# The first chunk reordered: dummy matmuls between its first real ones, the first z turn in two banks, the later z turns behind value matmuls, and V's pieces on both transfer queues

## The chip, the cores and the metric

The kernel runs on 1 core of a Trainium2 chip. The metric is the device time of one execution in microseconds. Nearly every run has the record of its granted TensorE clock. A "trace" is the profile of one execution.

The engines are named as in the profile: PE is TensorE, DVE is VectorE, ACT is ScalarE, POOL is GpSimd, SP is SyncE.

## The reference

Eight batches of squared-ReLU attention are gated by `u`, and all rows then go through a two-layer network.

```python
scores = z @ z.transpose(0, 2, 1) / S          # batch 8, S = 3008, z is 64 wide
attn = np.maximum(scores, 0.0) ** 2
x = (u * (attn @ v)).reshape(B * S, 256)
h = x @ w_in                                   # 256 -> 2048
out = (h / (1 + np.exp(-1.702 * h))) @ w_out   # 2048 -> 256
```

## The kernel before

For each batch the kernel takes S in six chunks, five of 512 columns and a last one of 448. Per pair of row blocks it makes scores on PE (`sc`), a ReLU on ACT (`rl`), a square on DVE (`a`), and value matmuls on PE (`o`). As the scores are symmetric, many squared blocks are reused: a DMA transpose on SP's queue turns `a` into `tt`, which later chunks use as weights.

Batch 0 has no batch ahead of it to hide its start. It loads z in groups of four blocks, casts them to 16 bits, turns them with PE transposes into a PSUM bank, and copies the bank to `ZT`. V comes through a staging tile `vst` that POOL casts. Everything below is this start (cuts marked).

```python
def warm_up(n):
    w = ps1.tile([P, CH], F32, name="w", tag="ps1")
    for k in range(n):
        pe.matmul(w, nil[:, :P], nil, start=(k == 0), stop=(k == n - 1))

def first_cast(g, by_act=False):           # zf (f32) -> zst (f16), two copies
    ...
        if by_act:
            act.activation(dst, src, AF.Copy, scale=1.0)
        else:
            dve.tensor_copy(dst, src)

def first_zt(g):                           # four PE transposes, then a copy to ZT
    zp = ps1.tile([P, CB, P], F16, name="zp", tag="ps1")
    for k in range(CB):
        pe.transpose(zp[:, k, :], z2[:, k, :, :], ident)
    def copies():
        ...
        if g != 1:
            act.activation(dst, src, AF.Copy, scale=1.0)
        else:
            dve.tensor_copy(dst, src)
    return copies

def load_u(b, i):                          # four transfers of 128 KB in pieces of 256 bytes
    eng = pool if b or i else sp
    ...

# the order of the start
first_z(0, CB, sp)                         # z group 0
first_z(CB, 2 * CB, act)                   # z group 1
for n0 in (0, VB):
    load_v(0, n0)                          # V blocks 0-3 and 4-7, on ACT's queue
first_z(2 * CB, 4 * CB, sp)                # z groups 2 and 3, ahead of all V on SP's queue
first_z(4 * CB, NJ, sp)
for n0 in range(2 * VB, NJ, VB):
    load_v(0, n0)                          # the rest of V, on SP's queue
warm_up(7)
for g in range(2):
    first_cast(g)
for copies in [first_zt(g) for g in range(2)]:
    copies()
posts = scores(0, [queue.pop(0) for _ in range(2)])
turns = []
for g in (2, 3):
    first_cast(g)
    turns.append(first_zt(g))
for post_ in posts:
    post_()                                # ReLU and square
turns[0]()
take(0, 1)                                 # one more pair of scores
...
# in chunk 0: turns[1]() at step 3; casts of groups 4 and 5 on ACT at steps 7 and 17, turns at 16 and 25
```

## Time and profile before

| | before |
|---|---|
| median of 3 runs (range) | 1192.46 us (1191.73 to 1192.65) |
| span of the profiled run | 1190.8 us |
| PE busy | 1183.7 us |
| PE waiting for other engines' results, in all | 3.3 us, all before 20 us |
| first value matmul | 8.40 us |
| first scores of chunk 1 | 25.14 us |

The busy line of the page (engine, busy us, share of the span, instructions):

```profile
PE 1183.7 (99%) x11427; PEld 722.6 (61%) x11427; DVE 820.6 (69%) x1315; ACT 830.5 (70%) x987; POOL 231.9 (19%) x325
```

PE is the bound, so only PE's idle time and its clock can be won at the start. The view by stretches shows both, in the columns named by its second line. PEclk is the granted clock.

```profile
core 0: us, PE busy (x) PEld busy (x) DVE busy (x) ACT busy (x) POOL busy (x), PEclk, DMA share, GB/s
4.45:7.86 3.41, 1.81 (x20) 0.85 (x18) 2.83 (x7) 2.65 (x4) 1.31 (x2) 1.00 1.09 352
7.86:11.27 3.41, 3.41 (x12) 0.77 (x10) 1.70 (x4) 2.65 (x4) 2.72 (x4) 0.50 1.10 346
11.27:25.00 13.73, 13.26 (x72) 4.66 (x70) 8.98 (x13) 11.82 (x17) 8.64 (x13) 1.00 1.18 205
```

In the first stretch PE was busy 1.81 of 3.41 us; in the next its clock was half, so 12 matmuls filled 3.41 us. The record of the clock begins only with the first full-speed window, at 4.45 us in this trace. Before that PEclk prints 1.00 although the warm-up matmuls start 0.427 us apart, against 0.216 for the same shape later. The timeline (start, us, engine, line, operation, output<-inputs, shape, count, idle time before it and what ended it) shows what PE waited for in the first of them:

```profile
4.72 0.60 ACT L141 ACTIVATE ZT<-zp 128x512 f16<-128x512 f16 x1 [1.21 <-PE zp L133]
5.38 0.61 PE L231 MATMUL sc<-ZT 64*128 64x512 f16 x4 [0.45 <-ACT ZT L141]
5.74 1.73 DVE L126 CAST zst<-zf 128x256 f16<-128x256 f32 x4
7.40 1.28 DVE L259 TENSOR_TENSOR a<-rl 128x1024 f16<-128x1024 f16 x2
7.53 0.40 PE L133 MATMUL zp<-ident,zst 128*128 128x128 f16 x4 [0.84 <-DVE zst L126]
8.40 1.03 PE L331 MATMUL o<-a,V 128*128 128x512 f16 x2
...
25.14 0.61 PE L231 MATMUL sc<-ZT 64*128 64x512 f16 x4
```

DVE casts z of groups 2 and 3 with hardly a wait for data (z landed at 5.72 us, 0.06 us after the copy before was done), then makes the first squares, and the value matmuls follow.

### The profile page before, as it was taken

Reading aid. Unit: us, or ns where it says so; the run is one execution under the profiler, and the core shown is the slowest. Engines: PE = TensorE matmul, PEld = TensorE weight load, DVE = VectorE, ACT = ScalarE, POOL = GpSimd, SP = SyncE. Lnnn points to the kernel's source line nnn. Section 1 sums busy time; section 2 is a strip of 40 time slices with the busy share of each in tenths; the row PEclk is TensorE's granted clock in tenths of the full one; section 3 lists DMA queues with packets and bytes.
Section 4 is the critical chain, followed back from the end, with each engine's and each line's share of the span. In section 5 each row is a group of like instructions: output and inputs, shape, how many; then the busy total and the mean of one; then the engine's idle time right before and its main releaser. Section 6 shows DMA issues by size and latency. Waiting matters only on the chain.

```text
span 1190.8 us, 27541 instructions
## 1 busy us (share of the span) xinstructions
PE 1183.7 (99%) x11427; PEld 722.6 (61%) x11427; DVE 820.6 (69%) x1315; ACT 830.5 (70%) x987; POOL 231.9 (19%) x325
## 2 busy tenths in 40 slices
PE   8999999999999999999999999999999999999998
PEld 3446765467754676546765478554775547855577
DVE  6788755777757775587765877558776487664776
ACT  7887865688656886478864787657876578672785
POOL 5243100331012320133101331014200142001000
PEclk9999999999999999999999999999999999999999
DMA  9996567666787667856778558886579855695012
GB/s 230 175 137 110 127 138 130 86 112 134 143 132 79 107 141 151 130 68 102 158 140 131 72 95 159 157 112 89 104 128 164 115 88 109 138 165 96 1 37 72
DMA packets 373021, 141.80 MB, mean 119 GB/s; under 512 B 315424, under 2 KB 366368, under 8 KB 372896
## 3 DMA queue, kind: packets, MB, share of 16 engines
q1 hardware_dynamic: 314256, 96.77, 45.1%
q0 software_dynamic: 57280, 42.03, 23.0%
q8 instruction: 89, 1.46, 0.5%
q10 hardware_dynamic: 1360, 1.25, 0.3%
q14 instruction: 36, 0.29, 0.1%
HBM read 60.29 MB, written 24.64 MB: 71 GB/s over the span
## 4 chain that ended last, share of the span: by engine, by line
PE 98%; ACT 0%; DMA 0%; DVE 0%; issue 0%; SPq 0%; ACTq 0%
PE o L331 40%; PE hg L372 27%; PE st L473 23%; PE sc L231 6%; PE yp L529 2%; DMA zf<-in_z_dram 0%; ACT rl L245 0%; DVE zst L126 0%; DVE a L259 0%; ACT ZT L141 0%; ACT zst L124 0%; DVE y L489 0%; SPq L109 0%; PE zp L133 0%; ACTq L245 0%
## 5 line engine op out<-in xcount | busy, mean ns | idle before, releaser
L380 ACT ACTIVATE gf<-hg 128x1024 f32<-128x1024 f32 (+1 forms) x384 | 385.8, 1005 | 138.0 <-PE hg L372 114.7
L245 ACT ACTIVATE rl<-sc 128x1024 f16<-128x1024 f32 x309 | 303.5, 1027 | 150.3 <-PE sc L231 147.5
L331 PEld LDWEIGHTS <-V 64*128 64x128 f16 (+1 forms) x4052 | 239.6, 94 | 235.4 <-issue 13.0
L372 PE MATMUL hg<-xt,W 128*128 128x512 f16 (+1 forms) x1408 | 354.6, 374 | 0.0
L384 DVE TENSOR_SCALAR gt<-gf 128x1024 f16<-128x1024 f32 (+1 forms) x320 | 223.2, 698 | 136.8 <-ACT gf L380 134.1
L331 PE MATMUL o<-a,V 64*128 64x512 f16 (+3 forms) x2286 | 303.8, 369 | 0.0
L259 DVE TENSOR_TENSOR a<-rl 128x1024 f16<-128x1024 f16 x274 | 188.7, 693 | 158.5 <-ACT rl L245 158.1
L193 POOL DMA_DIRECT2D uq<-in_u_dram x188 | 128.5, 691 | 612.2 <-PE sc L231 329.1
L331 PE MATMUL o<-tt,V 64*128 64x512 f16 (+1 forms) x1510 | 234.4, 377 | 0.0
L372 PEld LDWEIGHTS <-W 128*128 128x128 f16 x1536 | 139.3, 98 | 119.3 <-issue 2.6
L473 PEld LDWEIGHTS <-gt 128*128 128x128 f16 x2816 | 169.5, 98 | 31.8
L473 PEld LDWEIGHTS <-s 128*128 128x128 f16 x2112 | 127.8, 98 | 25.3 <-issue 0.3
L231 PE MATMUL sc<-ZT 64*128 64x512 f16 (+1 forms) x688 | 121.6, 367 | 1.2 <-ACT ZT L141 0.9
L473 PE MATMUL st<-WT,gt 128*128 128x128 f16 x1408 | 93.0, 219 | 0.0
L473 PE MATMUL st<-WT,s 128*128 128x128 f16 x1408 | 92.3, 219 | 0.0
L473 PE MATMUL st<-W,gt 128*128 128x128 f16 x1408 | 92.3, 219 | 0.0
L489 DVE SCALAR_TENSOR_TENSOR y<-st,uP 128x256 f32<-128x256 f32 x132 | 55.0, 419 | 21.6 <-PE st L473 10.9
L382 ACT ACTIVATE gt<-gf 128x1024 f16<-128x1024 f32 (+1 forms) x64 | 66.0, 1031 | 2.1
L348 DVE TENSOR_TENSOR xt<-o,ut 128x512 f16<-128x512 f32 x80 | 51.4, 683 | 22.7 <-PE o L331 22.7
L231 PEld LDWEIGHTS <-ZT 64*128 64x128 f16 x688 | 39.0, 94 | 45.0 <-issue 9.1
L483 ACT ACTIVATE uP<-st 128x256 f32<-128x256 f32 x132 | 49.7, 377 | 23.2 <-PE st L473 11.2
L446 DVE TENSOR_TENSOR s<-s,gt 128x1024 f16<-128x1024 f16 x88 | 60.3, 685 | 1.0
(51 smaller groups left out, 618.2 us busy)
## 6 DMA issues: line engine op xcount, KB each, us to landing
out_dram<-y SPq DMA_DIRECT2D x40, 512.0 KB, 3.3
uq<-in_u_dram POOLq DMA_DIRECT2D x156, 128.0 KB, 3.6
V<-in_v_dram POOLq DMA_DIRECT2D x35, 256.0 KB, 6.7
tt<-a SPq DMA_TRANSPOSE x232, 3.8
uq<-in_u_dram POOLq DMA_DIRECT2D x32, 112.0 KB, 5.2
vst<-in_v_dram SPq DMA_DIRECT2D x3, 512.0 KB, 5.8
out_dram<-y POOLq DMA_DIRECT2D x4, 384.0 KB, 3.2
zst<-in_z_dram POOLq DMA_DIRECT2D x7, 192.0 KB, 8.2
```

The costliest lines, as they stand in the source:

```text
L193: eng.dma_start(uq[k * QW:(k + 1) * QW, :n // QW].rearrange("t q c k -> t q (c k)"), src[:, :, cs])
L231: pe.matmul(sc[:, r, :m * P], zt[h, 2 * kp + r, :], zt[h, (qi + 1) * CB - m:(qi + 1) * CB, :], start=True, stop=True,)
L245: act.activation(rl, sc, AF.Relu, scale=csc)
L259: dve.tensor_tensor(a, rl, rl, ALU.mult)
L331: ins = pe.matmul(acc[c][:, :n], V16[b][h, j].rearrange("p (c k) -> p k c", k=NCC)[:, c], weights(b, i, j)[h], start=(k, m) == first[c], s ...
L372: pe.matmul(hg[:, e, :n], W1[:, c, ff * P:(ff + 1) * P], XT[b, i][:, c, :n], start=(c == 0), stop=(c == NCC - 1),)
L380: act.activation(gf[:, :, :n], hg[:, :, :n], AF.Gelu_apprx_sigmoid, scale=1.0 / FSC)
L382: act.activation(g, gf[:, :, :n], AF.Copy, scale=FSC)
L384: dve.tensor_scalar(g, gf[:, :, :n], FSC, None, ALU.mult)
L446: dve.tensor_tensor(s_, ST[b, k, "S1", h], a11, ALU.subtract)
L473: pe.matmul(bank[:, m, :], lhs()[:, f, m, :], right[:, ff, :], start=name in ("P1", "P2", "P5") and m == 0 and ff == 0, stop=ff == NFF // ...
L489: dve.scalar_tensor_tensor(y[:, :, o, c], ST[b, k, "bank" + x], 1.0 / FSC, ST[b, k, "after" + u_], ALU.mult, ALU.add,)
```

## The change

The intent: keep PE's clock up with dummy matmuls in the gaps, get the first scores sooner by splitting the first copy, get V's first block sooner by giving half of it to each queue, and let the first value matmuls go ahead of the turns of later z groups. The casts move from ACT to DVE. The core of the diff:

```diff
-    def warm_up(n):
-        w = ps1.tile([P, CH], F32, name="w", tag="ps1")
+    def keep_warm(n):
+        if "w" not in ZT:
+            ZT["w"] = ps1.tile([P, CH], F32, name="w", tag="ps1")
 ...
-            if by_act:
-                act.activation(dst, src, AF.Copy, scale=1.0)
-            else:
-                dve.tensor_copy(dst, src)
+            dve.tensor_copy(dst, src)
 ...
+        if g == 0:
+            zh = [ps1.tile([P, CB // 2, P], F16, name="zh", tag="ps1") for _ in range(2)]
+            ...
+                act.activation(dst[:, 0], zh[0].rearrange("d n p -> d p n"), AF.Copy, scale=1.0)
+                dve.tensor_copy(dst[:, 1], zh[1].rearrange("d n p -> d p n"))
 ...
-            if g != 1:
+            if g > 2:
 ...  load_v, batch 0
-            dst, eng = pa.tile(...), act if n0 < 2 * VB else sp
+            dst, eng = pa.tile(...), sp
+        if b == 0 and n0 == 0:
+            full = VB // 2
+            act.dma_start(dst[:, full:], v[b, full * P:VB * P].rearrange("(n p) c -> p n c", p=P))
 ...
-    FIRST_ZT, FIRST_CAST = {16: 4, 25: 5}, {7: 4, 17: 5}
+    FIRST_ZT, FIRST_CAST = {11: 3, 20: 4, 29: 5}, {2: 3, 15: 4, 24: 5}
-        0: {2: 1, 6: 2, 14: 2, 22: 2, 30: 2, 38: 2},
+        0: {2: 1, 8: 2, 16: 2, 25: 2, 33: 2, 40: 2},
 ...
-    first_z(2 * CB, 4 * CB, sp)
+    first_z(2 * CB, 4 * CB, act)
+    load_v(0, 2 * VB)
     first_z(4 * CB, NJ, sp)
-    for n0 in range(2 * VB, NJ, VB):
+    for n0 in range(3 * VB, NJ, VB):
         load_v(0, n0)
-    warm_up(7)
+    keep_warm(7)
 ...
+    keep_warm(1)
     posts = scores(0, [queue.pop(0) for _ in range(2)])
-    turns = []
-    for g in (2, 3):
-        first_cast(g)
-        turns.append(first_zt(g))
+    first_cast(2)
     for post_ in posts:
         post_()
-    turns[0]()
-    take(0, 1)
+    keep_warm(3)
+    posts = scores(0, [queue.pop(0)])
+    keep_warm(2)
+    ...
+    first_zt(2)()
+    posts[0]()
```

On the two hardware queues, z of groups 2 and 3 now stands behind V's first block and beside the next V blocks. Before, it stood ahead of V on SP's queue.

More of the change, by code (lines that the diff above doesn't have):

```diff
@@ L77 @@
     late, LATE = [], []
+    ZP = {}
     ZT, V16, UQ, UT, XT, unit, TT = {}, {}, {}, {}, {}, {}, {}
@@ L91, in behind @@
         tc.add_manual_dep(m.ins, sig.ins.name, SYNC, reason="row tiles of one bank")
-    def warm_up(n):
-        w = ps1.tile([P, CH], F32, name="w", tag="ps1")
+    def keep_warm(n):
+        if "w" not in ZT:
+            ZT["w"] = ps1.tile([P, CH], F32, name="w", tag="ps1")
         for k in range(n):
-            pe.matmul(w, nil[:, :P], nil, start=(k == 0), stop=(k == n - 1))
+            pe.matmul(ZT["w"], nil[:, :P], nil, start=(k == 0), stop=(k == n - 1))
     def first_z(n0, n1, eng):
@@ L117, in first_z, with first_cast @@
                 eng.dma_start(zf[h * SREM:(h + 1) * SREM, m1 + CB - 1, :], z[0, S0:S])
-    def first_cast(g, by_act=False):
+    def first_cast(g):
         m = g % CB * CB
@@ L122, in first_cast, with copies @@
             dst, src = ZT["st"][g // CB][:, m:m + CB, c, :], ZT["f"][g // CB][:, m:m + CB, :]
-            if by_act:
-                act.activation(dst, src, AF.Copy, scale=1.0)
-            else:
-                dve.tensor_copy(dst, src)
+            dve.tensor_copy(dst, src)
     def first_zt(g):
         z2 = ZT["st"][g // CB][:, g % CB * CB:(g % CB + 1) * CB]
-        zp = ps1.tile([P, CB, P], F16, name="zp", tag="ps1")
+        if g == 0:
+            zh = [ps1.tile([P, CB // 2, P], F16, name="zh", tag="ps1") for _ in range(2)]
+            for k in range(CB):
+                pe.transpose(zh[k // 2][:, k % 2, :], z2[:, k, :, :], ident)
+            def copies():
+                dst = ZT[0][:, :CB, :].rearrange("d n p -> d (n p)").rearrange("d (p h n) -> d h p n", h=2, n=CB // 2)
+                act.activation(dst[:, 0], zh[0].rearrange("d n p -> d p n"), AF.Copy, scale=1.0)
+                dve.tensor_copy(dst[:, 1], zh[1].rearrange("d n p -> d p n"))
+            return copies
+        zp = ZP[g] if g in ZP else ps1.tile([P, CB, P], F16, name="zp", tag="ps1")
         for k in range(CB):
@@ L172, in load_v @@
         if b == 0:
-            dst, eng = pa.tile([P, VB, D], F32, name="vst", tag="tt", bufs=14), act if n0 < 2 * VB else sp
+            dst, eng = pa.tile([P, VB, D], F32, name="vst", tag="tt", bufs=14), sp
         full = min(VB, NJ - 1 - n0)
+        if b == 0 and n0 == 0:
+            full = VB // 2
+            act.dma_start(dst[:, full:], v[b, full * P:VB * P].rearrange("(n p) c -> p n c", p=P))
         eng.dma_start(dst[:, :full, :], v[b, n0 * P:(n0 + full) * P].rearrange("(n p) c -> p n c", p=P))
-        if full < VB:
+        if n0 + VB == NJ:
             for h in range(2):
@@ L605 @@
         copies()
+    keep_warm(1)
     posts = scores(0, [queue.pop(0) for _ in range(2)])
-    turns = []
-    for g in (2, 3):
-        first_cast(g)
-        turns.append(first_zt(g))
+    first_cast(2)
     for post_ in posts:
         post_()
-    turns[0]()
-    take(0, 1)
+    keep_warm(3)
+    posts = scores(0, [queue.pop(0)])
+    keep_warm(2)
+    for g in (2, 3):
+        ZP[g] = ps1.tile([P, CB, P], F16, name="zp", tag="ps1")
+    first_zt(2)()
+    posts[0]()
     load_u(0, 1)
@@ L630 @@
                     load_u(0, 0)
-                if b == 0 and i == 0 and n == 3:
-                    turns[1]()
                 if b == 0 and i == 0 and n in FIRST_CAST:
-                    first_cast(FIRST_CAST[n], True)
+                    first_cast(FIRST_CAST[n])
                 if b == 0 and i == 0 and n in FIRST_ZT:
```

## The prediction

> **What bounds the kernel.** The tensor engine: the page's busy line gives PE 1183.7 of 1190.8 us. The list of waits shows PE waiting for other engines' results only before 20 us, 3.3 us in all. In the view by stretches, PE idles 2.8 us before 12 us and 3.7 us in the last 11; the change touches the first only. The same view grants PE a clock of 0.50 from 8 to 11 us (0.86 and 0.72 in the half microseconds on either side), 1.00 elsewhere: one slow stretch of some 3.4 us. In it value matmuls start 0.427 us apart, not 0.216. The Trainium skill, "TensorE: Matmul & The Clock Gate", Part 1, tells of such a gate: full clock after a busy window of about 3.4 us, half after an idle one. The trace agrees: from 4.5 to 7.5 us PE was busy 1.4 of 3.0.
>
> **What changes.**
> 1. Six 512-column dummies (0.216 us each) enter gaps where PE waits for ACT or DVE. They cost almost nothing and make that window about two thirds busy. If the clock holds, eight matmul slots gain 0.21 us each, 1.7 us; about 1 counts, since ACT (relu 1.02) and DVE (square 0.69) also pace these steps.
> 2. The first z turn's copy, 0.60 on ACT, becomes halves of some 0.38 on ACT and DVE: first scores at 5.15 instead of 5.37, 0.2 us.
> 3. ACT, busy 9.8 of 11 us from 12 to 23, loses the casts of groups 4 and 5 (1.4 us) and group 2's copy (0.60); DVE takes them. But the chain of scores, two relus (1.94), z copy (0.55) and next scores takes about 2.95 us, longer than eight value matmuls with scores (2.5). It occurs for groups 3, 4 and 5, before for two, leaving 0.2 to 0.5 us of PE idle time each. Net gain 0.4.
> 4. V's first block, on both queues, lands near 5.0 instead of 5.97, but z groups 2 and 3 now compete with later V: landing estimated at 6.5 to 7.1 instead of 5.72. Their cast stands before the first squares on DVE, so the first value matmul, 8.39 before, comes at 7.7 to 8.5. This takes back about 0.4.
>
> Bytes are unchanged. Transposed pieces land at least 4 us ahead of use in chunks 1 and 2 and PE has no later wait of size, so the shift should pass through to the end.
>
> **Sum.** 1.0 + 0.2 + 0.4 - 0.4 = 1.2 us gained, 0.1%. Chunk 1's first scores (25.14 before) come at 23.3 to 24.2.
>
> **Predicted: 1191.2 us, range 1190.1 to 1192.6** (8 in 10). Faster by over 2%: 0.003; within 2%: 0.994; slower: 0.003. All idle time at the head is under 1%.
>
> **What would show it.** Right: clock 1.00 throughout the head; value matmuls 0.216 apart from the first; chunk 1's first scores about 1.2 us earlier, and the same shift at the tail; PE waiting for z copies before the scores of groups 3 to 5; DVE waiting for the z DMA at 6 to 7 us. Wrong for step 1: half clock in some window. For step 4: no such DVE wait, or the first value matmul well outside 7.7 to 8.5.
>
> **What would make it wrong.** The dummies fail to fill the window and the clock drops (gain under 0.5 us, or a loss); the window's phase differs between runs, spreading single runs by about 1 us, as before's do (0.9); late z holds the squares and PE idles longer than before; u arrives too late for the faster steps.

## The result and the profile after

| | before | changed |
|---|---|---|
| median of 6 runs (range) | 1192.51 us (1191.72 to 1192.87) | 1193.69 us (1192.27 to 1197.57) |
| span of the profiled run | 1190.8 us | 1190.5 us |
| first scores | 5.38 us | 5.58 us |
| first value matmul | 8.40 us | 8.44 us |
| first scores of chunk 1 | 25.14 us | 24.84 us |

The prediction was a gain of 1.2 us, to 1191.2 us; the medians show a loss of 1.2 us. The ratio is 1.0016, with a 95% interval of 1.0001 to 1.003. A ratio is the mean time of one kernel's runs over that of the other's of the same rounds, so not quite the ratio of the medians quoted. The profiled execution was the fastest of the six, so its trace alone does not show the loss. The busy line:

```profile
PE 1184.3 (99%) x11433; PEld 721.7 (61%) x11433; DVE 823.6 (69%) x1321; ACT 828.5 (70%) x982; POOL 230.9 (19%) x325
```

The stretches that answer to those of before:

```profile
4.45:7.86 3.41, 3.26 (x20) 1.25 (x18) 1.73 (x6) 2.19 (x3) 1.17 (x2) 1.00 1.05 351
7.86:11.27 3.41, 3.26 (x20) 1.17 (x20) 3.41 (x5) 2.23 (x4) 3.10 (x4) 1.00 1.11 342
11.27:25.00 13.73, 12.92 (x72) 4.50 (x72) 11.66 (x19) 11.01 (x13) 8.54 (x12) 1.00 1.23 192
```

The clock held: 1.00 where it was 0.50. (In this trace its record begins at 5.72 us; until then the dummies still start 0.427 us apart.) But PE's busy time from 11.27 to 25 us fell from 13.26 to 12.92, so it idled more, and DVE's rose from 8.98 to 11.66. The timeline shows two new waits:

```profile
5.58 0.66 PE L244 MATMUL sc<-ZT 64*128 64x512 f16 x4
...
7.29 0.49 DVE L125 CAST zst<-zf 128x256 f16<-128x256 f32 x2 [1.34 <-DMA zf<-in_z_dram]
7.70 1.70 DVE L272 TENSOR_TENSOR a<-rl 128x1024 f16<-128x1024 f16 x2
...
8.44 0.59 PE L344 MATMUL o<-a,V 128*128 128x512 f16 x2
...
12.81 4.33 POOL L194 CAST V<-vst 128x512 f16<-128x512 f32 x5
...
14.34 1.31 DVE L125 CAST zst<-zf 128x256 f16<-128x256 f32 x2
15.57 2.10 DVE L272 TENSOR_TENSOR a<-rl 128x1024 f16<-128x1024 f16 x2
15.71 0.40 PE L143 MATMUL zp<-ident,zst 128*128 128x128 f16 x4 [0.54 <-DVE zst L125]
...
24.84 0.61 PE L244 MATMUL sc<-ZT 64*128 64x512 f16 x4
```

First, DVE waits 1.34 us for z of groups 2 and 3, and the squares stand behind that cast. Second, two casts take 1.31 us and two squares 2.10 us while POOL casts V: DVE is behind, and PE waits 0.54 us for a cast.

### The profile page after: what moved, and what is told of

It reads as the page before. It is cut to its first block, busy times and chain, and to the rows that moved or that the text cites. A ratio compares the mean times of both kernels' runs of the same rounds, so it can differ in the third digit from the quotient of the medians.

```text
span 1190.5 us, 27555 instructions
## 1 busy us (share of the span) xinstructions
PE 1184.3 (99%) x11433; PEld 721.7 (61%) x11433; DVE 823.6 (69%) x1321; ACT 828.5 (70%) x982; POOL 230.9 (19%) x325
## 4 chain that ended last, share of the span: by engine, by line
PE 98%; DVE 1%; DMA 0%; issue 0%; ACT 0%; ACTq 0%
PE o L344 40%; PE hg L385 27%; PE st L486 23%; PE sc L244 6%; PE yp L542 2%; DMA zf<-in_z_dram 0%; DVE a L272 0%; DVE zst L125 0%; DVE ZT L153 0%; ACT rl L258 0%; ACT ZT L151 0%; ACTq L187 0%; DVE y L502 0%; ACTq L111 0%; PE zp L143 0%
```

## The theories

Four were tried.

- **A, clock.** PE's clock falls to half after a window in which PE idles too much. The dummies prevent it, or fail to in some runs.
- **B, casts.** Casts on DVE beside POOL's V casts slow the squares, and with them the chain of scores.
- **C, late z.** z of groups 2 and 3 lands late behind V. Its cast holds the first squares on DVE and its turn holds PE.
- **D, crossing transfers.** Something after 25 us makes some executions 3 us or more slower. First form (D): the load of `u` for chunk 3 crosses the transposes that chunk 2 needs. Second form (D'): any `u` load on POOL's queue, in flight with the transposes on SP's queue, slows both.

All kernels below gave correct results. "Late runs" are those over 3 us above the lowest run of the same kernel in the same job. Each job ran its kernels and the kernel before on one chip: e1 to e4, e5 to e8, e9 to e12, e13 to e16 with e14, e18 and e19. Line numbers in profile lines differ by a few between kernels.

| run | what it is | median us | range us | late runs |
|---|---|---|---|---|
| e1 | changed kernel again | 1193.57 | 1192.60 to 1200.70 | 1 of 6 |
| e2 | changed, casts of groups 4, 5 on ACT | 1193.40 | 1192.85 to 1198.45 | 2 of 6 |
| e3 | changed, first transfers as before | 1192.36 | 1191.94 to 1198.68 | 2 of 6 |
| e4 | changed, no dummies in between | 1194.44 | 1193.69 to 1195.07 | 0 of 6 |
| (before, same job) | | 1192.55 | 1191.13 to 1196.47 | 3 of 11 |
| e5 | before with the dummies | 1194.79 | 1192.11 to 1199.04 | 3 of 6 |
| e6 | before with the changed transfers | 1194.84 | 1194.13 to 1195.82 | 0 of 6 |
| e7 | e3 with the casts on ACT | 1193.08 | 1191.84 to 1198.39 | 2 of 6 |
| e8 | before again | 1192.55 | 1191.44 to 1195.24 | 1 of 6 |
| (before, same job) | | 1192.84 | 1191.14 to 1197.18 | 2 of 11 |
| e9 | e7, u of chunk 3 held back | 1192.44 | 1191.90 to 1195.99 | 2 of 6 |
| e10 | changed, u of chunk 3 held back | 1193.99 | 1192.47 to 1194.72 | 0 of 6 |
| e11 | before, u of chunk 3 held back | 1192.64 | 1191.38 to 1197.44 | 1 of 7 |
| e12 | e9 without the first dummy | 1192.00 | 1191.18 to 1199.00 | 2 of 6 |
| (before, same job) | | 1192.63 | 1191.32 to 1198.35 | 3 of 11 |
| e13 | before, u on SP's queue | 1192.49 | 1192.41 to 1192.97 | 0 of 6 |
| e15 | changed, u on SP's queue | 1194.15 | 1192.97 to 1195.17 | 0 of 6 |
| e16 | e3, u on SP's queue | 1192.36 | 1191.95 to 1192.63 | 0 of 6 |
| e14 | e7 without the first dummy, u on SP's queue | 1191.84 | 1191.57 to 1192.28 | 0 of 6 |
| (before, same job) | | 1195.47 | 1191.81 to 1200.71 | 6 of 11 |
| e18 | e14 again | 1191.85 | 1191.63 to 1192.41 | 0 of 6 |
| e19 | e14 without its five dummies | 1191.85 | 1191.55 to 1193.37 | 0 of 6 |
| (before, same job) | | 1192.94 | 1191.61 to 1199.55 | 5 of 11 |

## The experiments

### e1: the changed kernel again

No edit.

> The changed kernel again, unedited, to see its spread and to get a second trace. All theories: median about 1193.5 us with single runs from 1192 to 1197 us, where the kernel before stays within 1191.7 to 1192.9. Theory A (clock): runs that are over 1193 us show a mean granted clock of 0.998 or less, and the trace a half-speed stretch after the first value matmul. Theory B (DVE beside POOL): the trace again shows casts of z groups 3 to 5 and squares at 0.69 and 1.09 us instead of 0.29 and 0.69, and no dependence on the clock. Theory C (late z): DVE waits for the z DMA of groups 2 and 3 until about 7.3 us, later in slow runs.

Measured: 1193.57 us, one run at 1200.70. The trace had the full clock after the warm-up and was yet 1.5 us slower than the first one. Its first value matmul came at 9.91 us, and DVE waited longer for z:

```profile
7.92 0.92 DVE L125 CAST zst<-zf 128x256 f16<-128x256 f32 x2 [2.08 <-DMA zf<-in_z_dram]
```

The squares before 11 us took 1.09 us each. Runs at 1193.5 to 1193.8 us had clocks of 0.999 to 1.000, so theory A does not explain the median; a late z that differs from run to run fits.

### e2: casts of groups 4 and 5 back on ACT

```diff
-            dve.tensor_copy(dst, src)
+            if g > 3:
+                act.activation(dst, src, AF.Copy, scale=1.0)
+            else:
+                dve.tensor_copy(dst, src)
```

> The changed kernel with the casts of z groups 4 and 5 back on ACT, as before; all else as changed. Theory B: DVE loses about 2.5 us of contended work from 14 to 18 us, the scores of groups 4 and 5 come earlier by about 0.5 us, and the median falls by 0.4 to 0.8 us, spread less. Theories A and C: no change in the median beyond 0.3 us.

Measured: 1193.40 us, with two late runs; the median moved by 0.17 us, inconclusive. In the trace the way from the scores at step 8 to chunk 1 took 13.81 us (11.39 to 25.20), against 14.19 in e1 (12.16 to 26.35): 0.4 us, a little less than the 0.5 us that was expected of the scores.

### e3: the first transfers as before

```diff
-            dst, eng = pa.tile(...), sp
-        if b == 0 and n0 == 0:
-            full = VB // 2
-            act.dma_start(dst[:, full:], v[b, full * P:VB * P]...)
+            dst, eng = pa.tile(...), act if n0 < 2 * VB else sp
 ...
-    first_z(2 * CB, 4 * CB, act)
-    load_v(0, 2 * VB)
+    first_z(2 * CB, 4 * CB, sp)
```

> The changed kernel with the order and queues of the first transfers of before (V's first two blocks on ACT's queue, z groups 2 and 3 on SP's ahead of V). Theory C: z of groups 2 and 3 lands near 5.7 instead of 7.3 us, squares start about 1 us earlier, the median falls by about 1 us and the spread to that of before. Theories A and B: the median moves by less than 0.3 us and the spread stays.

Measured: 1192.36 us, 1.2 us below e1. z landed at 4.98 us and the first value matmul came at 8.29. Theory C predicted this; A and B did not. The spread did not go: two late runs (1195.41 and 1198.68), against what theory C was given to expect.

### e4: no dummies in between

```diff
-    keep_warm(1)
     posts = scores(0, [queue.pop(0) for _ in range(2)])
 ...
-    keep_warm(3)
     posts = scores(0, [queue.pop(0)])
-    keep_warm(2)
```

> The changed kernel without the six dummies between the real matmuls; the seven at the start stay. Theory A (the dummies keep the clock, and it is lost only in some phases): nearly every run now has a half-speed stretch, mean clock 0.998 to 0.999, and the median rises by about 1 us. If the dummies are instead a cost by delaying real matmuls, the median falls by 0.3 us or more. Theories B and C: within 0.3 us of the changed kernel except for the clock.

Measured: 1194.44 us, 0.87 us above e1, mean clock 0.999 in four of six runs. The trace has a half-speed stretch from 9.4 to 12.8 us:

```profile
9.50:12.50 3.00, 2.86 (x8) 0.76 (x8) 3.00 (x6) 1.02 (x1) 2.44 (x4) 0.50 1.11 344
```

So with late z the dummies do what they are for.

### e5: the kernel before with the dummies alone

```diff
+    keep_warm(1)
     posts = scores(0, [queue.pop(0) for _ in range(2)])
+    keep_warm(3)
 ...
         turns.append(first_zt(g))
+        if g == 2:
+            keep_warm(2)
```

> The kernel before with the six dummies alone (one ahead of the first scores, three behind them, two between the turns of z groups 2 and 3); transfers, casts and turns as before. The first job showed the kernel before to fall into two groups, near 1191.4 us with a mean clock of 1.000 and near 1193 with 0.999. Theory A (the dummies keep the clock): only the lower group is left, median 1191.3 us, mean clock 1.000, first scores of chunk 1 near 24.0 us. If the dummies are worthless: median as before, both groups there.

Measured: 1194.79 us, three late runs; the lower three at 1192.1 to 1192.5, not 1191.3. Two of those three had the full clock. The trace had the full clock too and the first scores of chunk 1 at 24.40 us: 0.7 better than the trace of before that lost the clock (25.14), but 0.5 worse than the trace e8 of the same kernel that kept it by luck (23.89). Until 7.2 us the array was still at half speed in this run, and there a dummy takes up to 0.43 us and delays the turn behind it; the other two traces had reached full speed at 4.45 and 5.62 us, so they are not compared on equal terms. The expectation failed; the traces suggest, without proving it, that dummies are not free before the clock is up.

### e6: the kernel before with the changed transfers alone

> The kernel before with the changed order and queues of the first transfers alone. Theory C (late z of groups 2 and 3 holds DVE and with it the squares): z lands at 7.3 to 8.1 us instead of 5.0 to 5.7, the first squares start after 8.5 us instead of 7.4, and the median rises by 1.0 to 2.0 us. Theory B alone (casts on DVE are what costs): median within 0.3 us of before.

Measured: 1194.84 us, 2.0 us above the kernel before in the same job, with the smallest range of that job. z landed at 8.04 us. The list of PE's waits:

```profile
PE zp L133 <- DVE zst L126: 3.1, 1, 3.1
```

PE waited 3.1 us for the cast z, and lost its clock after it. This is theory C by itself, without any cast moved.

### e7: e3 with the casts on ACT

> The changed kernel with both the order of the transfers and the casts of groups 4 and 5 as before; what stays of the change are the dummies, the split first turn and the later turns. Theories B and C together: the lower runs come at 1191.2 to 1191.6 us, against 1192.0 with the old transfers alone; first scores of chunk 1 near 24.8 us instead of 25.2. Theory C alone: as with the old transfers alone, within 0.2 us.

Measured: 1193.08 us with two late runs; the lowest two 1191.84 and 1191.94, above the expected band and on another chip than e3, so the times do not decide it. The traces do: first scores of chunk 1 at 24.39 us against 25.16 in e3, 0.77 us, with the first value matmul at 8.29 in both. In e3 (first) two casts between squares take 1.31 us; in e7 (second) they are gone and DVE waits for ACT instead:

```profile
12.63 2.11 DVE L269 TENSOR_TENSOR a<-rl 128x1024 f16<-128x1024 f16 x2
14.66 1.31 DVE L125 CAST zst<-zf 128x256 f16<-128x256 f32 x2
```

```profile
12.63 2.11 DVE L272 TENSOR_TENSOR a<-rl 128x1024 f16<-128x1024 f16 x2
15.20 2.12 DVE L272 TENSOR_TENSOR a<-rl 128x1024 f16<-128x1024 f16 x2 [0.47 <-ACT rl L258]
```

### e8: the kernel before again

No edit.

> The kernel before, unedited, to sample its groups of runs and to get a second trace. All theories: two groups, near 1191.4 us where the trace grants full clock from the first value matmul on, near 1192.5 to 1193 where it has a half-speed stretch between 5 and 13 us; occasional runs over 1195 us, as the first job had for both kernels.

Measured: 1191.44 to 1195.24 us. The profile caught the run of 1195.24 us. The head kept its clock, chunk 1 began at 23.89 us, 1.25 us earlier than in the first trace of this kernel, and at 40 us PE ran into a transposed block that had not landed:

```profile
PE o L331 <- DMA tt<-a: 2.0, 1, 2.0
```

The half-speed stretch that followed went from 43.2 to 46.6 us. So a faster head can be paid back later, and the late runs are not of the changed kernel alone. Here a transpose issued at 35.6 us landed at 42.7, with the `u` load of chunk 3 (issued from 35.2 on) in between. That is theory D.

### e9, e10, e11: u of chunk 3 held back

```diff
     def load_u(b, i):
         eng = pool if b or i else sp
+        if (b, i) == (0, 3):
+            held = const.tile([P, 1], F16, name="held")
+            pool.tensor_copy(held, XT[0, 1][:, 1, :1])
```

The copy waits for chunk 1's gated output, and the load stands behind it on POOL.

> The changed kernel with the transfers and the ACT casts of before, and the load of u for chunk 3 held back until chunk 1's gated output is written (near 39 us instead of 35); its data is used near 60 us. Theory D (the earlier the head, the more the u load crosses the transposes that chunk 2 needs; PE then waits near 41 us and loses the clock there): no run more than 2.5 us above the lowest, where 2 of 6 were without the hold; lowest runs as before the hold, 1191.8 us. If the slow runs come from elsewhere: 1 to 3 of 6 runs still near 1197 to 1199 us.

> The changed kernel with only that hold added. Theory D: median 1193 us (the late z stays), no run over 1195.5 us. Otherwise: runs up to 1197 or 1200 us as in both rounds of the changed kernel.

> The kernel before with only that hold added. Theory D: two groups near 1191.4 and 1193 us stay (clock of the head), but no run over 1195 us, where 6 of 34 were. Otherwise about one run in six over 1195 us.

Measured: late runs in e9 (1195.79 and 1195.99) and in e11 (1197.44), none in e10, whose head is the slowest of the three. Theory D in this form fell. But two profiles caught late runs. In e11, the kernel before with the hold, the hold was in force (that load was issued at 40.0 us), and PE still waited, longer:

```profile
39.98 0.38 PE L334 MATMUL o<-tt,V 64*128 64x512 f16 x2
44.89 1.15 PE L334 MATMUL o<-tt,V 64*128 64x512 f16 x6 [4.53 <-DMA tt<-a]
```

The transfer view of the stretch from 28 to 38 us shows why. Queue q0 carries the `u` load of chunk 2 from POOL, q1 the transposes from SP. The columns are packets, MB, and the time the packets took as a share of 16 engines. First e11, then the first trace of the kernel before:

```profile
DMA packets 2355, 1.06 MB, mean 106 GB/s; under 512 B 2227, under 2 KB 2227, under 8 KB 2355
q1 hardware_dynamic: 2163, 0.54, 63.4%
q0 software_dynamic: 192, 0.52, 55.7%
```

```profile
DMA packets 6694, 2.15 MB, mean 215 GB/s; under 512 B 6565, under 2 KB 6565, under 8 KB 6693
q1 hardware_dynamic: 6501, 1.62, 87.6%
q0 software_dynamic: 192, 0.52, 26.9%
```

The same 192 packets of `u` took twice the engine time, and the transposes moved a third of the bytes while still occupying 63%. In the first trace the two came one after the other: from 29 to 31 us only `u` moved. So it is mainly the `u` load of chunk 2: in e11 a transpose issued at 22.41 us, just ahead of that load (22.64), landed only at 38.88. The transpose that PE waited for was issued at 39.42 and landed at 44.84 us, beside the held load of chunk 3 (from 39.98). As the bytes of `u` are the same in both traces, it is not their amount; that it is the crossing is argued here from one late trace. In e9 the late run had another victim of crowded transfers, a weight block (issued at 58.07 us and landed at 70.07, while a transpose issued at 56.05 landed at 71.39):

```profile
PE hg L388 <- DMA W<-in_moe_w_in_dram: 2.8, 1, 2.8
```

### e12: e9 without the first dummy

```diff
-    keep_warm(1)
     posts = scores(0, [queue.pop(0) for _ in range(2)])
```

> As the first kernel of this job, without the one dummy ahead of the first scores. Its trace showed that dummy at 0.43 us, as the clock is still at half there, and the first scores behind it at 5.57 us. Expected: first scores at 5.30 to 5.45 us and the lowest runs 0.1 to 0.2 us lower, 1191.6 us; with theory D no run over 1194.5 us.

Measured: median 1192.00 us, two late runs, the lowest 1191.18. The first scores came at 5.40 us, inside the expected band; but in e9's trace they came at 5.44 us with the dummy, so its removal gained little there. The late runs did not go, as in e9.

### e13, e15, e16, e14: u of the first batch on SP's queue

This puts the `u` loads in line with the transposes. The first weight load was kept at its time by binding it to a later chunk, since POOL no longer waits for `u` ahead of it. For e13 (kernel before), e15 (changed kernel) and e16 (e3) the edit is this; e14 is e7 with it and without the first dummy.

```diff
-        eng = pool if b or i else sp
+        eng = pool if b else sp
 ...
-            pool.tensor_copy(hold, XT[0, 1][:, 0, :1])
+            pool.tensor_copy(hold, XT[0, 2][:, 0, :1])
```

> The kernel before, with all u loads of the first batch on SP's queue, in line with the transposes, and the first weight load bound to chunk 2's output instead of chunk 1's, so that it keeps its time. Theory D' (u pieces and transposes in flight together from two queues slow each other): no wait of PE for a transposed block, no run over 1194 us out of 6; two groups stay, near 1191.4 and 1193. If the slow runs have another cause: one in six still over 1195.

> The changed kernel with the same move of u. Theory D': no run over 1195 us; median 1193.3 us, the late z and the casts staying.

> The changed kernel with the first transfers as before and the same move of u. Theory C: 1.0 to 1.5 us below the changed kernel with that move, median 1192.0 us, no slow group.

> As the run above, with the casts of groups 4 and 5 back on ACT and without the dummy ahead of the first scores. Theory B: 0.6 to 0.9 us below it, median 1191.3 us, no slow group; that would be 1 us below the median of the kernel before. Without B: 0.1 to 0.2 us below it, for the dummy.

Measured: no late run in 24, while the kernel before, on the same chip in the same rounds, had 6 of 11. Kernels with `u` on POOL's queue had 36 late runs of 140, and those with `u` on SP's queue 0 of 36. This is what theory D' predicts. It does not yet single out the crossing, because the move changes more than one thing: the queue is of another kind (q1 hardware_dynamic instead of q0 software_dynamic in the transfer view), and in line behind the transposes the `u` load of chunk 2 is issued at 35.09 us in e13 instead of 24.25 in the first trace of before. No run tried `u` on ACT's queue, or all of `u` held back on POOL's. One more trace speaks for the crossing: in e14 the weight blocks still go by POOL's queue, and the transposes issued beside them at 54.67 and 56.01 us took 8.0 and 9.0 us to land, against a median of 3.3 from 28 to 38 us; PE did not wait for them. The price of the move is in e13: the six runs lie in one group at 1192.4 to 1193.0 us, not in the two expected, and the lower group of before on that chip began at 1191.81. One run of e15 came at 1195.17, just over its limit; its profile is that run, and shows no wait for a transposed block but the lost clock below. The median of e15, 1194.15 us, was expected at 1193.3.

With the late runs gone the parts could be told apart, on one chip:

- e15 against e13: the whole change costs 1.66 us (1194.15 against 1192.49).
- e15 against e16: the changed transfers cost 1.79 us of it. That is theory C, above what was expected (1.0 to 1.5); the two ranges do not meet (1192.97 to 1195.17 against 1191.95 to 1192.63).
- e16 against e13: all the rest of the change gives 0.13 us, which is within the spread of both (1191.95 to 1192.63 against 1192.41 to 1192.97).
- e16 against e14: casts on ACT and one dummy less give 0.52 us. Theory B was given 0.6 to 0.9, the dummy 0.1 to 0.2; the size of B in time is thus some 0.3 to 0.4 us, an estimate, as the worth of the dummy was not measured apart.

The stretches of e15 and e16 show the path of theory C, including its second step. First e15, then e16:

```profile
7.90:11.50 3.60, 1.54 (x10) 0.66 (x11) 3.12 (x5) 0.97 (x2) 2.89 (x4) 1.00 1.08 344
11.50:15.00 3.50, 3.50 (x12) 0.79 (x11) 2.85 (x5) 1.55 (x2) 2.95 (x5) 0.51 1.07 279
```

```profile
7.90:11.50 3.60, 3.60 (x22) 1.30 (x21) 3.38 (x7) 2.73 (x4) 2.61 (x4) 1.00 1.10 348
11.50:15.00 3.50, 3.41 (x19) 1.13 (x17) 3.50 (x5) 3.01 (x5) 3.27 (x5) 1.00 1.23 244
```

In e15 z landed at 8.36 us. PE, in order, stood before the turn of that group and was busy only 1.54 of 3.60 us, and then lost the clock for the next stretch, in spite of the dummies, which all lie before that point:

```profile
PE zp L143 <- DVE zst L125: 1.5, 1, 1.5
```

This trace is the slowest of its six runs. The lost clock is not the rule: two of the six runs have a mean clock of 0.998, and the other four, at 1192.97 to 1194.15 us, round to 1.000. All four still lie above the slowest run of e16 (1192.63), so late z costs time with the clock kept, too. The DVE lines of e15, then e16:

```profile
8.38 0.91 DVE L125 CAST zst<-zf 128x256 f16<-128x256 f32 x2 [2.54 <-DMA zf<-in_z_dram]
9.21 2.10 DVE L272 TENSOR_TENSOR a<-rl 128x1024 f16<-128x1024 f16 x2
```

```profile
5.86 0.48 DVE L125 CAST zst<-zf 128x256 f16<-128x256 f32 x2
7.28 0.69 DVE L269 TENSOR_TENSOR a<-rl 128x1024 f16<-128x1024 f16 x1 [0.94 <-ACT rl L255]
```

In e15 the first ReLU was done at 6.85 us, and its square began at 9.21, after the cast that stood before it. The late cast also pushes the squares into the time of POOL's next V casts: 2.10 us for two, where early ones take 0.69 us each.

### e18, e19: e14 again, and without its dummies

e18 has no edit to e14. e19 takes out `keep_warm(3)` and `keep_warm(2)`.

> The version e14 again, unedited. If it is as good as its first draw: median 1191.5 to 1192.1 us, no run over 1193 us, and below the median of the kernel before of the same rounds.

> The version e14 without its five dummies between the real matmuls. Theory A: the clock falls to half for one window of 3.4 us below 15 us in most runs (mean clock 0.999 or less), and the median is 0.8 to 1.3 us higher, near 1192.9 us. If the dummies are worth nothing without late z: within 0.2 us of the run before it.

Measured: e18 at 1191.85 us, as the first draw. e19 at 1191.85 us as well, mean clock 1.000 in all six runs, so the expectation failed: with z early and only one later group turned ahead of the value matmuls, the first real work kept the window busy enough without dummies (in the trace 2.79 of 3.41 us from 6.67 us on). They are worth nothing in the median there. Two of six runs of e19 were higher (1192.77 and 1193.37).

e14 and e18 are the best version: ratios to the kernel before of 0.9966 (0.9940 to 0.9992) and 0.9978 (0.9955 to 1.0000). Most of that is the missing late runs of before. Its medians are 0.03 and 0.24 us above the lowest runs of before (1191.81 and 1191.61 in the two jobs); against before with `u` on SP's queue it is 0.65 us better.

## Why the prediction was wrong, point by point

1. **PE bounds the kernel, and only the head can change it.** Right. The whole difference is about 0.1%.
2. **The dummies keep the clock (1.0 us).** The mechanism is right, the size only in part. The first trace has the clock at 1.00 from 5.72 us on, as predicted, and with late z the dummies save 0.87 us (e4 against e1). But the prediction took the lost clock of one trace for the rule: of the 36 runs of the kernel before in the five jobs that were not late, 20 have a mean clock of 1.000, and these had next to nothing to win. The first scores of chunk 1 in e5 came 0.7 us earlier than in a trace that had lost the clock, and 0.5 later than in one that had kept it; in e19 they are worth nothing. Dummies also cannot help behind a 1.5 us wait that comes after them (e15). The Trainium skill, "TensorE: Matmul & The Clock Gate", Part 1, describes the free-running window of 3413 ns; the traces agree: every half-speed stretch within the heads and at the later waits lasted 3.41 us, and the first full-speed window began anywhere from 4.00 us (e2) to 7.21 us (e5), the phase that the prediction named. Where the prediction says that the trace agrees with half clock "after an idle one", it goes too far: PE was busy 1.81 us of that window (see the last section).
3. **The split first copy (0.2 us).** Nearly nothing in most traces. Without a dummy ahead of them the first scores came at 5.39 us with the split (e14) and at 5.48 without it (e13). With the dummy, at half clock, they came at 5.58. Where the array was at full speed early, the split did give its 0.2 us: 5.11 us in e2 (from 4.00 us, dummy and all) against 5.30 in e11 (from 4.29, no split).
4. **Casts off ACT (+0.4 us net).** The wrong sign: putting two back on ACT, with one dummy less, gained 0.52 us. The prediction counted ACT's relief and not the cost on DVE. Its own trace of before shows that cost: two of DVE's casts took 0.70 us beside a POOL cast, the others 0.29. Nor did it count that the squares on DVE, which PE needs, would stand behind these casts and be slowed too. Of the PE waits for copies, those ahead of the scores of groups 3 and 5 came at the small end: the last value matmul and the scores start 0.51 and 0.53 us apart, against 0.31 where nothing is waited for. At group 4 PE waited for the DVE cast instead, 0.54 us.
5. **Late z (-0.4 us).** This is the step that failed and that turns a gain into a loss: the mechanism was right, and the term of the sum was 0.4 us where 1.79 was measured (e15 against e16). The prediction said: "landing estimated at 6.5 to 7.1 instead of 5.72. Their cast stands before the first squares on DVE, so the first value matmul, 8.39 before, comes at 7.7 to 8.5. This takes back about 0.4." Measured, z landed at 7.26 us in the first trace and at 7.56 to 8.53 in the other six traces with these transfers (e1, e2, e4, e6, e10, e15). The first value matmul came at 8.44 us in the first trace, inside the predicted band, and at 9.15 to 10.93 in the other six; that the profiled run confirmed this step was luck. Three things were missed. The estimate was a mean flow, while a transfer is done when the last of its parts has landed: in the first trace 13 of the 16 parts of z had landed from 5.62 to 5.84 us, the last at 7.26. In e15 and e6 the whole transfer was later, with the first part at 6.99 and 6.90 us; what decides between the two is not shown. The Trainium skill, "DMA: Bandwidth & Descriptors", section "Why a DMA increments its semaphore by 16 and not by 1", says that only the full count means that all data landed, and the trace agrees: the cast began at 7.29 us. The squares were pushed into POOL's next casts (1.09 us each instead of 0.69). And PE's wait could cost the clock again, as it did in two of e15's six runs.
6. **The shift passes through to the end.** Right in the first trace (0.30 us earlier at chunk 1, 0.3 at the end), wrong as a rule. "Transposed pieces land at least 4 us ahead of use" was read from one trace. In another of the same kernel (e8) PE waited 2.0 us for one, and 4.5 us in e11, where one load was held back. These late runs are not what made the changed kernel slower: it had 2 of 12, before 20 of 67. They widened its range, and hid the differences of 0.5 to 2 us until `u` left POOL's queue.
7. **The sum.** Predicted 1.0 + 0.2 + 0.4 - 0.4 = 1.2 us gained. On one chip, without late runs, the parts are 0.13 us gained by points 2 to 4 together and 1.79 us lost by point 5: 1.66 us lost. Against its sum the prediction thus missed 2.9 us, in about equal parts: 1.4 in point 5, and 1.5 in points 2 to 4, which were to give 1.6 and gave nothing clear of the spread. What stays open: which of points 2 to 4 fell short by how much, as they were not all tested one by one without late runs; and why two queues in flight together sometimes crawl and sometimes take turns; the runs show that it happens and how to avoid it, not what decides it.

## What to carry to other kernels

When transfers are reordered, ask which instruction waits for the piece that moved back and what stands behind it in that engine's order; here z of two groups, landing at 7.26 to 8.53 us instead of 4.61 to 5.72, held the squares and the turn behind it, while V's first block, in the first trace at 5.15 us instead of 5.97, could not be used before those squares. A slack read from one trace is a single draw, so look at the spread of the runs, and catch a trace of a slow one, before trusting it. If two streams of transfers slow each other, putting them in line on one queue can be worth more than tuning the head, as it was here (36 late runs of 140 against none of 36).

## What the Trainium skill lacked or had wrong

- "TensorE: Matmul & The Clock Gate", Part 1, says that the clock is lost after an idle window (a later section of the page tells of a kernel that lost it by frequent short idle times). Here no idle window was needed. In 22 windows of 3.41 us at full clock that the traces were asked for (in the heads, and at the later waits of e8, e9 and e11), PE was busy 0.33 to 1.81 us in the seven that were followed by half clock, and 1.97 to 3.41 us in the fifteen that were not. The page gives no such share. It is no sharp threshold of the profile's busy time either: one more window of e11, from 38.43 us, had 1.93 us busy and one at the end of before, from 1185.46 us, 1.79, and both kept the clock. So the windows part at somewhat over half busy in these traces, and not closer.
- "DMA: Bandwidth & Descriptors", section "Queues, rings and completion order", says that each engine takes turns between queues packet by packet. It does not say what a transpose stream and a stream of 256-byte pieces from another queue do to each other: the same 0.52 MB took 55.7% instead of 26.9% of the engines' time, and the transposes moved 0.54 MB instead of 1.62 in 10 us (e11 against before). In line on one queue, 0 of 36 runs were late instead of 36 of 140; the kind of the queue and the time of the loads changed with it.
- "GPSIMD Engine Reference", section 1, names the contention with VectorE for the shared interfaces without a size; no other page gives times for these instructions either. In the first trace of the changed kernel a square with two inputs took 1.09 us instead of 0.69 beside a POOL cast, a cast on DVE 0.69 instead of 0.29, and POOL's cast 1.07 instead of 0.61.
